# Attention of the first two blocks moved ahead of the first layer's products, with outputs and scores of a visit in PSUM banks of their own

## The chip, the core and the metric

The kernel runs on one core of a Trainium2 chip. The metric is device time in microseconds (us) of one execution; the times shown for the kernel before are a median of three runs and a profile of one more execution.

## What is computed

Three layers follow each other. A retention attention over 4 batches, 8 heads, 768 positions and a head size of 64 gives 3072 tokens of 512 features. A first MLP takes them through `w_in` (512 x 2048) and `w_out`, a second through `w_in2` (512 x 1024) and `w_out2`:

```python
state = gamma * state + k_t (outer) v_t;  y_t = scale * q_t @ state     # attention, per head
h = x @ w_in;   x1 = (h - tanh(h)) @ w_out                              # first MLP
h = x1 @ w_in2; solu = h * softmax(h); out = (layernorm(solu) * g_ln) @ w_out2
```

All inputs are 4-byte floats, but the weights come as 8-byte words that the kernel has to turn into floats itself.

## The kernel before

**Blocks and units.** The sequence is cut into 6 blocks of 128 positions. A block has 4 units, one for each batch, so there are 24 units. A unit holds 8 heads; its recurrence is done by chunks of 64 positions, as products of 64x64 tiles on TensorE. Unit k needs: scores of q and k (`sc`), the growth of the state from k and scaled v (`gn`), the product of q with the old states (`fr`), and the product of the masked scores with scaled v (`y`). Each of the four has 16 products. The trace shows one 64x64 product as two matmul records and two weight loads.

**A visit.** `unit(ko, ks)` (L228) does the outputs `fr` and `y` of one unit, `ko`, and the scores and growth of a later unit, `ks`. It takes four PSUM banks, `one` (two) and `two` (two). In the kernel before each bank holds a half for the outputs and a half for the scores: `one` has `fr` and `sc`, `two` has `y` and `gn`. `prepare(k)` (L207) scales v (`vs`) and q (`qs`, on GpSimd, L223). With `early` the eight scalings of v are on ScalarE (L214), otherwise one is on GpSimd (L218). After the products VectorE makes `pr` (masked scores, L278), `sb` and `sa` (states, L274 and L282), ScalarE copies `fr` to `xf` (L292), VectorE adds `y` to it (L295), and `split_x` (L302) splits the sum into a rounded part `xh` (ScalarE, L307) and a rest `xl` (L308).

**First MLP.** All products of the MLPs are 128x128 by 128x512 and come three to one: high by high, high by low, low by high. `products_h(s, f)` (L313) makes 12 of them for block s and tile f of `w_in` (16 tiles). `less_tanh` (L324) takes the tanh on ScalarE and `g = h - tanh(h)` on VectorE. `products_y` (L338) has 12 products for a tile of `w_out`. A weight tile is decoded in four stages (`Decoder`, L149): its load (`raw`, L116), an absolute value on ScalarE (L122), four operations on VectorE (L129 to L136), and a rounding on ScalarE with a subtraction on VectorE (L145, L146). Decoded tiles stay in SBUF.

**The order around the change.** Units 0 to 3 come first, with two tiles of `w_in` decoded between them. Then a loop over n (L408) does block 0's products for tile n, and block 1's, `BEHIND` = 5 tiles later:

```python
less_tanh(products_h(0, n, ps_y, "y"), g2[n][:, 0, :])          # block 0
if n <= B: ... unit(k - 1 ..., k ..., True)                     # units 4 to 7
elif LATER <= n <= LATER + B: ... unit(..., True, True)         # units 8 to 11
if n >= BEHIND: less_tanh(products_h(1, f, ps_y, "y"), g2[f][:, 1, :])
```

After that loop come the `products_y` of both blocks (L460), the blocks 2 to 5 one by one (L490), and the second MLP (L586). A scheduler puts the instructions of each engine in a fixed order when the program is built; each engine takes its own in that order. The loads `z` (inputs of the units) and `raw` are issued by SyncE (SP), the tables `tab` by ScalarE. Buffers come from pools: 44 of one size (`t4`: `z`, `raw`, decoded weights, x, g), 17 of a smaller one (`t2`).

Of the kernel before, what the change touches and what calls it, by code (L numbers as in the profile page):

```python
# [36 lines left out]
P = 128  # L37
# [11 lines left out]
BEHIND = 5  # L49
LATER = 6  # L50
# [42 lines left out]
def body(ctx: ExitStack, tc, z, w_in, w_out, w_in2, w_out2, g_ln, cst, tab, out):  # L93
# [89 lines left out]
    zero = cpool.tile([P, NP, D], F32, name="zero")  # L183
# [23 lines left out]
    def prepare(k, early):  # L207
        c = k // B
        v = t2([P, H, D], F32, "vs")
        src = zv[k][:, 1, :, :].rearrange("q p (h d) -> q (p h) d", h=2)  # L210
        c0 = C_VS + c * H
        if early:
            for h in range(H):
                nc.scalar.activation(  # L214
                    v[:, h, :], src[:, h, :], AF.Copy, scale=con[:, c0 + h : c0 + h + 1]
                )
        else:
            nc.gpsimd.tensor_tensor(  # L218
                v, src, con[:, c0 : c0 + H].unsqueeze(2).to_broadcast([P, H, D]), ALU.mult
            )  # L220
        vs[k] = v
        qs[k] = t2([P, NP, P], F32, "qs")
        nc.gpsimd.tensor_tensor(  # L223
            qs[k].rearrange("q p t -> q (p t)"),
            zq[k][:, 0, :, :].rearrange("q p t -> q (p t)"), tb[c][1], ALU.mult,
        )

    def unit(ko, ks, early, hold=False, pool=ps_r, tag="r"):  # L228

        if ks is not None:  # L230
            c = ks // B
            if ks not in vs:
                prepare(ks, early)
            kq, kv, v = zq[ks], zv.pop(ks), vs[ks]

        one = [pool.tile([P, 2, 4 * D], F32, tag=tag, name="one") for _ in range(2)]
        two = [pool.tile([P, 2, 4 * D], F32, tag=tag, name="two") for _ in range(2)]
        if ko is not None:
            q, vo, po, st = qs.pop(ko), vs.pop(ko), pt.pop(ko), (sa.pop(ko), sb.pop(ko))
            fr = [t[:, 0, :].rearrange("q (i t) -> q i t", i=2) for t in one]  # L240
            y = [t[:, 0, :].rearrange("q (h i t) -> q h i t", h=2, i=2) for t in two]
            products([
                (
                    fr[h][rows(col(2 * i + odd, h)), i, rows(ab)],
                    st[ab][rows(h), 2 * i + odd, :], q[rows(h), 2 * i + odd, rows(ab)],
                )
                for i in range(2) for ab in range(2) for odd in range(2) for h in range(2)
            ])
        if ks is not None:
            sc, gn = ([t[:, 1, :].rearrange("q (p t) -> q p t", p=NP) for t in w] for w in (one, two))  # L250
# [9 lines left out]
        if ko is not None:  # L260
            products([
                (
                    y[ab][rows(col(p, h)), h, p // 2, :], vo[rows(ab), 2 * p + h, :],
                    po[rows(ab), h, p, :],
                )
                for p in range(NP) for ab in range(2) for h in range(2)
            ])
        if ks is not None:
            sb[ks] = stp.tile([P, NP, D], F32, tag="sb", name="sb", bufs=3)
            if c == 0:  # L270
                sa[ks] = zero
                nc.scalar.copy(sb[ks], gn[0])
            else:
                nc.vector.tensor_tensor(sb[ks], sa[ks], gn[0], ALU.add)  # L274
# [4 lines left out]
            pt[ks] = pr  # L279
            if c < NC - 1:  # L280
                sa[ks + B] = stp.tile([P, NP, D], F32, tag="sa", name="sa")
                nc.vector.tensor_tensor(sa[ks + B], sb[ks], gn[1], ALU.add)  # L282
        if ko is not None:
            c, b = divmod(ko, B)
            if hold:
                if b % 2 == 0:
                    xc[b // 2] = t4([P, 2, 2, 2, P], F32, "xc")
                xf = xc[b // 2][:, b % 2, :, :, :]
            else:
                xf = t2([P, 2, 2, P], F32, "xf")  # L290
            for h in range(2):
                nc.scalar.copy(xf[:, h, :, :], fr[h])  # L292
            xa = xf.rearrange("q h i t -> q (h i) t")
            for ab in range(2):
                nc.vector.tensor_tensor(  # L295
                    xa[:, :, rows(ab)], xa[:, :, rows(ab)],
                    y[ab].rearrange("q h i t -> q (h i) t"), ALU.add,
                )
            if not hold:
                split_x(c, b, xf, nc.vector if early else nc.gpsimd)  # L300

    def split_x(c, b, xf, eng):  # L302
        if b == 0:
            xt[c] = [[t4([P, 2, SB], F32R, f"x{n}") for _ in range(2)] for n in "hl"]
        for h in range(2):
            xh, xl = (xt[c][n][h][:, :, b * P : (b + 1) * P] for n in range(2))
            nc.scalar.copy(xh, xf[:, h, :, :])  # L307
            eng.tensor_tensor(xl, xf[:, h, :, :], xh.bitcast(F32), ALU.subtract)  # L308
# [74 lines left out]
    spare = dict(pool=ps_y, tag="y")  # L383
    dec1.n = NF1
    load_units(1)
    nc.sync.dma_start(out=con, in_=cst[:, :C_IDENT])
    dec1.to(0, 1)
    load_units(4)
    dec1.to(0, 2)
    load_units(5)  # L390
    dec1.to(0, 3)
    nc.gpsimd.memset(zero, 0.0)
    unit(None, 0, True)
    for st in range(1, 4):
        dec1.to(st, 1)
    unit(None, 1, True, **spare)
    prepare(2, True)
    unit(0, 2, True)
    prepare(3, True)
    unit(1, 3, True, **spare)  # L400
    unit(2, None, True)
    dec1.to(1, 2)
    prepare(4, True)
    unit(3, None, True, **spare)
    for st in range(1, 4):
        dec1.to(st, 2)
    g2 = {}
    for n in range(NF1 + BEHIND):  # L408
        if n < NF1:
            while dec1.at[3] < n + 1:  # L410
                dec1.step()
            g2[n] = t4([P, 2, SB], F32, "g")
            less_tanh(products_h(0, n, ps_y, "y"), g2[n][:, 0, :])

        if n <= B:
            k = B + n
            load_units(min(k + 2, 2 * B))
            if n < B - 1:
                prepare(k + 1, True)
            unit(k - 1 if n else None, k if n < B else None, True)  # L420
        elif LATER <= n <= LATER + B:
            k = 2 * B + n - LATER
            load_units(min(k + 2, 3 * B))
            unit(k - 1 if n > LATER else None, k if n < LATER + B else None, True, True)
        elif n == LATER - 1:
            load_units(2 * B + 1)
            nc.sync.dma_start(out=gl, in_=g_ln)
        if n >= BEHIND:
            f = n - BEHIND
            less_tanh(products_h(1, f, ps_y, "y"), g2[f][:, 1, :])  # L430
        if n < NF1 - 3:
            dec1.step()
        else:

            dec1.n = 2 * NF1
            for st, ahead in enumerate((1, -1, -1, -2)):
                dec1.to(st, max(NF1, NF1 + min(4 - st, n - NF1 + 3 + ahead)))
            if n < NF1:
                dec1.to(3, min(NF1, n + 2))
# [6 lines left out]
    split_g(0)  # L446
    py2 = [
# [3 lines left out]
    for n in range(NF1 + 1):  # L451
# [9 lines left out]
        if n % 2 == 0 and NF1 // 2 <= n < NF1:  # L461
            b = (n - NF1 // 2) // 2
            split_x(2, b, xc[b // 2][:, b % 2, :, :, :], nc.vector)
# [26 lines left out]
    for n, (s, f) in enumerate(steps):  # L490
# [4 lines left out]
        if n in visits:  # L495
            unit(*visits[n], False)
            load_units((visits[n][1] or NU) + 2)
# [156 lines left out]
```

## Time and profile before

| | |
|---|---|
| median of 3 runs | 921.95 us (919.96 to 922.29) |
| the profiled execution | 922.72 us, of it 920.8 us in the profile's span |
| TensorE matmul busy | 885.1 us, 96% of the span; 6720 matmuls and 6720 weight loads |
| VectorE, ScalarE, GpSimd busy | 440.4, 307.6, 182.8 us |
| share of TensorE in the chain that ended last | 93% |
| mean granted TensorE clock | 0.983 |
| DMA | 73.48 MB, mean 80 GB/s |

The chain that ended last is followed back from the last instruction, at each step to what released it. A wait named "issue" is one for which the profile shows no releaser. PE is TensorE, DVE VectorE, ACT ScalarE, POOL GpSimd, SP SyncE. A matmul's shown duration overlaps the next one's, so costs of matmuls are taken from a stretch and its count.

### The profile page before, as it was taken

Reading aid. Unit: us, or ns where it says so; the run is one execution under the profiler, and the core shown is the slowest. Engines: PE = TensorE matmul, PEld = TensorE weight load, DVE = VectorE, ACT = ScalarE, POOL = GpSimd, SP = SyncE. Lnnn points to the kernel's source line nnn. Section 1 sums busy time; section 2 is a strip of 40 time slices with the busy share of each in tenths; the row PEclk is TensorE's granted clock in tenths of the full one; section 3 lists DMA queues with packets and bytes.
Section 4 is the critical chain, followed back from the end, with each engine's and each line's share of the span. In section 5 each row is a group of like instructions: output and inputs, shape, how many; then the busy total and the mean of one; then the engine's idle time right before and its main releaser. Section 6 shows DMA issues by size and latency. Waiting matters only on the chain.

```text
span 920.8 us, 16028 instructions
## 1 busy us (share of the span) xinstructions
PE 885.1 (96%) x6720; PEld 728.1 (79%) x6720; DVE 440.4 (48%) x884; ACT 307.6 (33%) x633; POOL 182.8 (20%) x185
## 2 busy tenths in 40 slices
PE   4678999999999999999999999999999999999998
PEld 4555788788888888888888888888888888888886
DVE  3596865996122333222322249973544444444442
ACT  4553633654011121111211133531533333333332
POOL 2101100000024433333333310010222222222210
PEclk9787999999999999999999999999999999999999
DMA  9905112532141123112311026305111111000000
GB/s 358 397 7 183 52 44 69 161 92 92 29 132 47 48 70 95 44 47 69 92 48 46 24 76 199 92 12 142 42 46 46 47 46 47 23 23 23 24 23 35
DMA packets 35640, 73.48 MB, mean 80 GB/s; under 512 B 3184, under 2 KB 15600, under 8 KB 35568
## 3 DMA queue, kind: packets, MB, share of 16 engines
q1 hardware_dynamic: 17712, 56.73, 18.5%
q10 hardware_dynamic: 17856, 15.73, 5.3%
q8 instruction: 53, 0.87, 0.4%
q14 instruction: 19, 0.16, 0.1%
HBM read 59.86 MB, written 12.58 MB: 79 GB/s over the span
## 4 chain that ended last, share of the span: by engine, by line
PE 93%; DVE 3%; ACT 2%; DMA 1%; issue 1%; SPq 0%; ACTq 0%; DVEq 0%
PE py L344 29%; PE ph L320 28%; PE po L578 14%; PE ph L530 14%; PE one L204 2%; PE ptr L565 2%; PE two L204 2%; ACT vs L214 1%; DMA con<-cst 1%; DVE wf L136 1%; DVE xf L295 1%; ACT xf L292 0%; DVE wf L133 0%; DVE wf L129 0%; DVE w L146 0%
## 5 line engine op out<-in xcount | busy, mean ns | idle before, releaser
L320 PE MATMUL ph<-xh,w 128*128 128x512 f32 x768 | 254.2, 400 | 10.4 <-ACT xh L307 5.4
L344 PE MATMUL py<-gh,w 128*128 128x512 f32 x768 | 248.4, 391 | 1.2 <-ACT gh L332 1.2
L320 PEld LDWEIGHTS ph<-xh,w 128*128 128x128 f32 x768 | 147.6, 193 | 42.9 <-ACT xh L307 5.7
L344 PEld LDWEIGHTS py<-gh,w 128*128 128x128 f32 x768 | 144.1, 188 | 31.7 <-ACT gh L332 1.6
L327 DVE TENSOR_TENSOR g<-ph,th 128x512 f32<-128x512 f32 x96 | 66.2, 689 | 204.5 <-ACT th L326 204.2
L320 PE MATMUL ph<-xl,w 128*128 128x512 f32 x384 | 153.1, 399 | 0.0
L344 PE MATMUL py<-gl,w 128*128 128x512 f32 x384 | 150.8, 393 | 0.0
L326 ACT ACTIVATE th<-ph 128x512 f32<-128x512 f32 x96 | 57.4, 598 | 246.8 <-PE ph L320 227.1
L530 PE MATMUL ph<-w,y 128*128 128x512 f32 x576 | 134.9, 389 | 0.0
L530 PEld LDWEIGHTS ph<-w,y 128*128 128x128 f32 x576 | 108.0, 188 | 22.4
L335 POOL TENSOR_TENSOR gl<-g,gh 128x512 fp32r<-128x512 f32 x48 | 61.7, 1286 | 307.9 <-DVE gh L334 286.7
L578 PE MATMUL po<-w,uh 128*128 128x512 f32 x384 | 120.4, 395 | 0.0
L379 POOL TENSOR_TENSOR y<-yl,y 128x512 fp32r<-128x512 f32 x24 | 42.2, 1760 | 260.9 <-ACT y L378 232.5
L320 PEld LDWEIGHTS ph<-xl,w 128*128 128x128 f32 x384 | 74.0, 193 | 15.7
L536 DVE TENSOR_REDUCE nmx<-ph 128x1 f32<-128x1024 f32 x24 | 29.4, 1225 | 117.7 <-PE ph L530 117.7
L344 PEld LDWEIGHTS py<-gl,w 128*128 128x128 f32 x384 | 72.1, 188 | 15.2
L578 PEld LDWEIGHTS po<-w,uh 128*128 128x128 f32 x384 | 70.6, 188 | 13.6
L578 PE MATMUL po<-w,ul 128*128 128x512 f32 x192 | 75.3, 392 | 0.0
L539 ACT ACTIVATE ex<-ph,nmx 128x1024 f32<-128x1024 f32 x24 | 26.8, 1117 | 132.5 <-DVE nmx L536 132.5
L223 POOL TENSOR_TENSOR qs<-z,tab 128x512 f32<-128x512 f32 x24 | 31.9, 1331 | 86.5 <-DMA tab<-tab 36.4
L541 DVE SCALAR_TENSOR_TENSOR ex<-ph,ex 128x1024 f32<-128x1024 f32 x24 | 29.4, 1225 | 29.8 <-ACT ex L539 29.8
L578 PEld LDWEIGHTS po<-w,ul 128*128 128x128 f32 x192 | 36.0, 188 | 7.6
(64 smaller groups left out, 850.7 us busy)
## 6 DMA issues: line engine op xcount, KB each, us to landing
z<-z SPq DMA_DIRECT2D x48, 512.0 KB, 5.8
raw<-w_in SPq DMA_DIRECT2D x24, 512.0 KB, 7.5
raw<-w_out SPq DMA_DIRECT2D x24, 512.0 KB, 3.6
y1d<-ysb ACTq DMA_DIRECT2D x24, 256.0 KB, 3.3
yl<-y1d SPq DMA_DIRECT2D x24, 256.0 KB, 3.3
out<-ob ACTq DMA_DIRECT2D x24, 256.0 KB, 2.1
tab<-tab ACTq DMA_DIRECT2D x12, 256.0 KB, 3.3
ident<-cst SPq DMA_DIRECT2D x1, 64.0 KB, 9.4
```

The lines of the kernel that those rows point to most:

```text
L204: nc.tensor.matmul(o, a, b, start=True, stop=True, skip_group_check=True)
L223: nc.gpsimd.tensor_tensor(qs[k].rearrange("q p t -> q (p t)"), zq[k][:, 0, :, :].rearrange("q p t -> q (p t)"), tb[c][1], ALU.mult,)
L320: nc.tensor.matmul(ph, a[:, k, :], x, start=n == 0, stop=n == 3 * NK - 1)
L326: nc.scalar.activation(th, ph, AF.Tanh)
L327: nc.vector.tensor_tensor(g, ph, th, ALU.subtract)
L335: eng_l.tensor_tensor(gl_, g, gh.bitcast(F32), ALU.subtract)
L344: nc.tensor.matmul(py[e], a[:, cols], x, start=f == 0 and n == 0, stop=f == NF1 - 1 and n == 2)
L379: nc.gpsimd.tensor_tensor(yo, t, yh.bitcast(F32), ALU.subtract)
L530: nc.tensor.matmul(ph[:, half, :], a[:, k, :], b, start=n == 0, stop=n == 3 * NK - 1)
L536: nc.vector.tensor_reduce(nmx, phf, AX.X, ALU.max, negate=True)
L541: nc.vector.scalar_tensor_tensor(ex, phf, 1.0, ex, ALU.mult, ALU.mult, accum_out=us)
L578: nc.tensor.matmul(po, a[:, f, :], b, start=n == 0, stop=n == 3 * NF2 - 1)
```

## The change

All eight units of blocks 0 and 1 run before the loop over the tiles of `w_in`. Then each step n of the loop has both blocks' products for tile n, with units 8 to 11 in steps 3 to 7 (`LATER` = 3). Only the products of block 0 with tile 0 stand earlier, between the units 3 and 4. A visit now puts outputs and scores into banks of their own: `out` (two, with `fr` and `y`) and `sc` (two, with `sc` and `gn`), does the outputs first, and up to unit 7 the score banks come from the pool `ps_y`. Of the first block's units the product with the zero state is gone (8 of 64 products in a unit, with the tile of zeros). For units 0 to 7 half of v's scaling moves from ScalarE to GpSimd, and one of two `xl` from VectorE to GpSimd. In `split_x`, `engs` names an engine for each half. Cut to its core:

```diff
-BEHIND = 5
-LATER = 6
+LATER = 3
...
-    def prepare(k, early):
+    def prepare(k, own):
...
+        for h in range(own):
+            nc.scalar.activation(
+                v[:, h, :], src[:, h, :], AF.Copy, scale=con[:, c0 + h : c0 + h + 1]
+            )
+        if own < H:
             nc.gpsimd.tensor_tensor(
-                v, src, con[:, c0 : c0 + H].unsqueeze(2).to_broadcast([P, H, D]), ALU.mult
+                v[:, own:, :], src[:, own:, :],
+                con[:, c0 + own : c0 + H].unsqueeze(2).to_broadcast([P, H - own, D]), ALU.mult,
             )
...
-    def unit(ko, ks, early, hold=False, pool=ps_r, tag="r"):
+    def unit(ko, ks, hold=False, pool=ps_r, tag="r", engs=None):
...
-        one = [pool.tile([P, 2, 4 * D], F32, tag=tag, name="one") for _ in range(2)]
-        two = [pool.tile([P, 2, 4 * D], F32, tag=tag, name="two") for _ in range(2)]
         if ko is not None:
...
+            w = [ps_r.tile([P, 2, 4 * D], F32, tag="r", name="out") for _ in range(2)]
+            fr = [t[:, 0, :].rearrange("q (i t) -> q i t", i=2) for t in w]
+            y = [t[:, 1, :].rearrange("q (h i t) -> q h i t", h=2, i=2) for t in w]
+
+            steps = range(2) if c else (1,)
...
+            else:
+                for h in range(2):
+                    nc.scalar.copy(xf[:, h, :, rows(1)], fr[h][:, :, rows(1)])
+                nc.scalar.copy(xa[:, :, rows(0)], ya[0])
...
         if ks is not None:
-            sc, gn = ([t[:, 1, :].rearrange("q (p t) -> q p t", p=NP) for t in w] for w in (one, two))
+            c = ks // B
+            kq, kv, v = zq[ks], zv.pop(ks), vs[ks]
+            w = [pool.tile([P, 2, 4 * D], F32, tag=tag, name="sc") for _ in range(2)]
+            sc, gn = ([t[:, n, :].rearrange("q (p t) -> q p t", p=NP) for t in w] for n in range(2))
...
+    both = dict(engs=(nc.vector, nc.gpsimd))
...
+    for k in range(2 * B):
+        load_units(min(k + 6, 2 * B))
+        if k + 2 < 2 * B:
+            prepare(k + 2, H // 2)
+        if k == B:
+            step_h(0, 0)
+        unit(k, k + 2 if k + 2 < 2 * B else None, **both, **(spare if k < B else {}))
+        if k >= B:
+            dec1.to(0, k - B + 2)
+    dec1.step()
+    nc.sync.dma_start(out=gl, in_=g_ln)
+    for n in range(NF1):
+        while dec1.at[3] < n + 1:
+            dec1.step()
+        for b in range(2):
+            if n or b:
+                step_h(n, b)
+
+        if LATER <= n <= LATER + B:
...
```

`step_h(n, b)` is `less_tanh(products_h(b, n, ps_y, "y"), g2[n][:, b, :])`.

**TensorE at the start.** `ph` are products with `w_in`; `one<-qs` and `two<-pr` (before), `out<-qs` and `out<-pr` (now) are outputs; rows from `z` are scores and growth. Before, from the outputs of units 2 and 3 on:

```order
L204 MATMUL two<-pr,vs 64x64 x16
L204 MATMUL one<-qs,zero 64x64 x4
L204 MATMUL one<-qs,sb 64x64 x4
L204 MATMUL one<-qs,zero 64x64 x4
L204 MATMUL one<-qs,sb 64x64 x4
L204 MATMUL two<-pr,vs 64x64 x16
L320 MATMUL ph<-xh,w 128x512 x2
L320 MATMUL ph<-xl,w 128x512
```

Now, from the outputs of unit 3 and the scores of unit 5 on:

```order
L202 MATMUL out<-qs,sb 64x64 x8
L202 MATMUL out<-pr,vs 64x64 x16
L202 MATMUL sc<-z 64x64 x16
L202 MATMUL sc<-vs,z 64x64 x16
L319 MATMUL ph<-xh,w 128x512
L319 MATMUL ph<-xl,w 128x512
```

Twelve `ph` follow there, then the outputs of unit 4; and after the outputs of unit 7 the dense stream of `ph` begins:

```order
L202 MATMUL out<-qs,sb 64x64 x4
L202 MATMUL out<-qs,sa 64x64 x4
L202 MATMUL out<-qs,sb 64x64 x4
L202 MATMUL out<-pr,vs 64x64 x16
L319 MATMUL ph<-xh,w 128x512 x2
L319 MATMUL ph<-xl,w 128x512
```

Units 4 to 7 moved ahead of all `ph` but twelve.

**ScalarE at the end of the units.** `vs` is v's scaling, `xf` and `xh` belong to a unit's outputs, `wf` and `w` to the decoding of `w_in`, `th` is the first tanh. Before, around units 2 and 3, the end of block 0:

```order
L292 COPY xf<-one 128x256
L122 ACTIVATE wf<-raw 128x512
L214 ACTIVATE vs<-z,con 128x64 x4
L292 COPY xf<-one 128x256
L214 ACTIVATE vs<-z,con 128x64 x4
L145 CAST w<-wf 128x512
L307 CAST xh<-xf 128x2x128 x2
L292 COPY xf<-one 128x256 x2
L307 CAST xh<-xf 128x2x128 x2
L326 ACTIVATE th<-ph 128x512
```

Now, at the end of block 1, from the scaling for unit 7 on:

```order
L212 ACTIVATE vs<-z,con 128x64 x4
L262 COPY xf<-out 128x256 x2
L306 CAST xh<-xf 128x2x128 x2
L262 COPY xf<-out 128x256 x2
L306 CAST xh<-xf 128x2x128 x2
L262 COPY xf<-out 128x256
L121 ACTIVATE wf<-raw 128x512 x3
L262 COPY xf<-out 128x256
L306 CAST xh<-xf 128x2x128 x2
L144 CAST w<-wf 128x512 x2
```

Where one decoding stood beside unit 2's copies, the starts of three stand between the two copies of unit 7's outputs.

**SyncE's loads at the start.** Before:

```order
L194 DMA z<-z 128x1024 x2
L386 DMA con<-cst 128x49
L116 DMA raw<-w_in 128x1024
L194 DMA z<-z 128x1024 x6
L116 DMA raw<-w_in 128x1024
L194 DMA z<-z 128x1024 x2
L116 DMA raw<-w_in 128x1024
```

Now, in the same queue, after the first five units' loads and one `raw`:

```order
L192 DMA z<-z 128x1024 x6
L115 DMA raw<-w_in 128x1024 x6
L192 DMA z<-z 128x1024 x4
L115 DMA raw<-w_in 128x1024
L192 DMA z<-z 128x1024 x2
```

The inputs of all eight units stand ahead of the second tile of `w_in`.

## Rows read from the trace of the kernel before

**Rows 1.** Chain of waits in order of time: start, us, what.

```profile
79.53 6.91 PE ph L320 x17
...
121.52 43.76 PE ph L320 x192
165.30 0.60 ACT th L326
...
166.46 87.33 PE py L344 x384
...
282.70 1.09 PE one L204 x64
...
284.92 1.09 PE two L204 x64
```

**Rows 2.** Busy time in stretches: length, engines (instructions), clock, DMA share, GB/s.

```profile
0.00:10.00 10.00, 1.45 (x37) 1.27 (x40) 0.76 (x2) 2.00 (x4) 1.77 (x6) 1.00 0.84 295
10.00:42.00 32.00, 19.89 (x494) 17.82 (x493) 17.45 (x36) 17.56 (x62) 7.87 (x6) 0.79 1.03 406
60.00:70.00 10.00, 8.32 (x192) 6.83 (x182) 9.20 (x21) 5.31 (x18) 0.00 (x0) 1.00 0.01 3
80.00:90.00 10.00, 10.00 (x61) 7.47 (x60) 3.62 (x4) 0.54 (x2) 2.40 (x2) 0.73 0.92 358
```

**Rows 3.** Timeline, TensorE: the two waits that nothing in the profile released.

```profile
26.75 0.27 PE L204 MATMUL two<-vs,z 64*64 64x64 f32 x2 [2.25 <-issue]
33.23 0.38 PE L204 MATMUL one<-qs,sb 64*64 64x64 f32 x4 [3.33 <-issue]
```

**Rows 4.** Busy time as in rows 2, from the start to each wait.

```profile
0.00:24.60 24.60, 11.50 (x348) 10.63 (x349) 8.39 (x14) 11.74 (x40) 7.11 (x10) 1.00 0.96 361
0.00:29.95 29.95, 14.66 (x474) 13.69 (x475) 11.97 (x24) 14.01 (x48) 8.38 (x11) 0.96 0.97 369
```

**Rows 5.** DMA queues: whole span, then 16 to 17, 24 to 26, 30 to 32 us.

```profile
q8 instruction: 53, 0.87, 0.4%
...
q8 instruction: 1, 0.02, 6.8%
...
q8 instruction: 1, 0.02, 3.4%
...
q8 instruction: 1, 0.02, 3.3%
```

**Rows 6.** Groups by line and shape: count, busy us, mean ns, idle before.

```profile
L307 ACT CAST xh<-xf 128x256 fp32r<-128x256 f32 x40 | 14.3, 404 | 33.3 <-DVE xf L295 28.6 <-DMA tab<-tab 4.7
L292 ACT COPY xf<-one 128x256 f32<-128x256 f32 x40 | 13.6, 371 | 54.4 <-DVE pr L278 32.4 <-POOL vs L218 18.6 <-PE one L204 3.3
L122 ACT ACTIVATE wf<-raw 128x512 f32<-128x512 f32 x48 | 31.4, 668 | 9.7 <-PE py L344 8.8 <-DVE w L146 0.9
L146 DVE TENSOR_TENSOR w<-wf,w 128x512 fp32r<-128x512 f32 x48 | 35.7, 743 | 2.0 <-ACT w L145 1.7
L129 DVE TENSOR_SCALAR wf<-wf 128x512 f32<-128x512 f32 x48 | 21.8, 455 | 9.3 <-ACT wf L122 9.3
L327 DVE TENSOR_TENSOR g<-ph,th 128x512 f32<-128x512 f32 x96 | 66.2, 689 | 204.5 <-ACT th L326 204.2
L295 DVE TENSOR_TENSOR xf<-xf,two 128x256 f32<-128x256 f32 x40 | 15.7, 414 | 3.2 <-ACT xf L292 3.2
L218 POOL TENSOR_TENSOR vs<-z,con 128x512 f32<-128x512 f32 x12 | 12.5, 1043 | 0.0
L308 POOL TENSOR_TENSOR xl<-xf,xh 128x256 fp32r<-128x256 f32 x24 | 17.2, 736 | 27.0 <-ACT xh L307 27.0
L223 POOL TENSOR_TENSOR qs<-z,tab 128x512 f32<-128x512 f32 x24 | 31.9, 1331 | 86.5 <-DMA tab<-tab 36.4 <-PE two L204 22.0 <-DVE w L146 11.9
```

**Rows 7.** Timeline, ScalarE, VectorE and GpSimd: v's scalings, then two that overlap.

```profile
9.28 2.02 ACT L214 ACTIVATE vs<-z,con 128x64 f32<-128x64 f32 x8
...
16.51 1.27 POOL L223 TENSOR_TENSOR qs<-z,tab 128x512 f32<-128x512 f32 x1 [1.05 <-DMA z<-z]
16.69 1.64 DVE L146 TENSOR_TENSOR w<-wf,w 128x512 fp32r<-128x512 f32 x1 [0.68 <-ACT w L145]
```

More of the change, by code (lines that the diff above doesn't have):

```diff
@@ L226, in prepare @@
         )
-    def unit(ko, ks, early, hold=False, pool=ps_r, tag="r"):
[L230 to L234, printed above, removed]
-        one = [pool.tile([P, 2, 4 * D], F32, tag=tag, name="one") for _ in range(2)]
-        two = [pool.tile([P, 2, 4 * D], F32, tag=tag, name="two") for _ in range(2)]
-        if ko is not None:
-            q, vo, po, st = qs.pop(ko), vs.pop(ko), pt.pop(ko), (sa.pop(ko), sb.pop(ko))
-            fr = [t[:, 0, :].rearrange("q (i t) -> q i t", i=2) for t in one]
-            y = [t[:, 0, :].rearrange("q (h i t) -> q h i t", h=2, i=2) for t in two]
+    def unit(ko, ks, hold=False, pool=ps_r, tag="r", engs=None):
+        if ko is not None:
+            c, b = divmod(ko, B)
+            q, v, po, st = qs.pop(ko), vs.pop(ko), pt.pop(ko), (sa.pop(ko, None), sb.pop(ko))
+            w = [ps_r.tile([P, 2, 4 * D], F32, tag="r", name="out") for _ in range(2)]
+            fr = [t[:, 0, :].rearrange("q (i t) -> q i t", i=2) for t in w]
+            y = [t[:, 1, :].rearrange("q (h i t) -> q h i t", h=2, i=2) for t in w]
+            steps = range(2) if c else (1,)
             products([
@@ L259, in unit @@
             ])
[L260 to L274, printed above, removed]
             pr = t2([P, 2, NP, D], F32, "pr")
@@ L279, in unit @@
             pt[ks] = pr
+            sb[ks] = stp.tile([P, NP, D], F32, tag="sb", name="sb", bufs=3)
+            if c == 0:
+                nc.scalar.copy(sb[ks], gn[0])
+            else:
+                nc.vector.tensor_tensor(sb[ks], sa[ks], gn[0], ALU.add)
             if c < NC - 1:
@@ L282, in unit, with split_x @@
                 nc.vector.tensor_tensor(sa[ks + B], sb[ks], gn[1], ALU.add)
[L283 to L302, printed above, removed]
+    def split_x(c, b, xf, engs):
         if b == 0:
@@ L386, in body @@
     nc.sync.dma_start(out=con, in_=cst[:, :C_IDENT])
+    load_units(2)
     dec1.to(0, 1)
-    load_units(4)
-    dec1.to(0, 2)
     load_units(5)
-    dec1.to(0, 3)
-    nc.gpsimd.memset(zero, 0.0)
-    unit(None, 0, True)
+    prepare(0, H // 2)
+    unit(None, 0, **spare)
+    prepare(1, H // 2)
     for st in range(1, 4):
         dec1.to(st, 1)
[L396 to L406, printed above, removed]
+    unit(None, 1, **spare)
     g2 = {}
[L408 to L411, printed above, removed]
+    def step_h(n, b):
+        if b == 0:
             g2[n] = t4([P, 2, SB], F32, "g")
[L413 to L421, printed above, removed]
+        less_tanh(products_h(b, n, ps_y, "y"), g2[n][:, b, :])
@@ L422, in body @@
             k = 2 * B + n - LATER
+            if n == LATER:
+                load_units(k + 1)
+                prepare(k, H)
             load_units(min(k + 2, 3 * B))
[L424 to L431, printed above, removed]
+            if n < LATER + B - 1:
+                prepare(k + 1, H)
@@ L432, in body @@
+            unit(k - 1 if n > LATER else None, k if n < LATER + B else None, True)
+        if n < NF1 - 4:
             dec1.step()
@@ L435, in body @@
             dec1.n = 2 * NF1
[L436 to L439, printed above, removed]
+            m = n - (NF1 - 4)
+            for st, ahead in enumerate(((1, 2, 2, 2), (0, 1, 2, 2), (0, 1, 1, 2), (0, 0, 1, 2))):
+                dec1.to(st, max(NF1 if st < 3 else min(NF1, n + 2), NF1 + ahead[m]))
     gs = {}
@@ L495, in body @@
         if n in visits:
-            unit(*visits[n], False)
-            load_units((visits[n][1] or NU) + 2)
+            ko, ks = visits[n]
+            if ks is not None:
+                prepare(ks, 0)
+            unit(ko, ks)
+            load_units((ks or NU) + 2)
             next_y(n)
```

38 lines of the change are left out of this document (28 added, 10 removed).

## The prediction

> **What bounds the kernel now.** I read the chain of waits in order of time first, then the busy time by stretches, then the waits of TensorE and the DMA queues in the first 50 us. In the chain [rows 1] the reader is to see one point: from 79.53 us on it is TensorE's own work almost without a break, through the last product with `w_in` (its tanh starts at 165.30) and the products with `w_out`. 192 products took 43.76 us, 0.228 us each, and a unit's outputs and scores 1.09 + 1.09 = 2.18 us. That work is the same after the change, so time can only come out of the stretch before 79.5 us, where TensorE waits, or be lost there.
>
> What it waits for before 79.5 us has two parts. From 60 to 70 us VectorE is busy 9.20 of 10 us [rows 2]: the decoding of `w_in`, the units 4 to 7 and their splits meet on VectorE while each step gives TensorE work for one block only. Before that, from 10 to 42 us, the DMA engines are full (share 1.03, 406 GB/s [rows 2]), and TensorE stops twice, 2.25 and 3.33 us, for nothing that the profile shows, in the middle of a unit's products [rows 3]. At the first stop it had executed 348 matmuls and 349 weight loads, at the second 474 and 475 [rows 4]: 697 and 949, 252 apart. The queue named q8 moved 53 packets and 0.87 MB in all [rows 5], 16.4 KB each, for TensorE's 6720 matmuls and 6720 weight loads: one packet for 254 of these 13,440. So I read the stops as TensorE waiting for its own instructions: one packet stands in 16 to 17 us, one in 24 to 26 and one in 30 to 32 us [rows 5]. TensorE went on at 26.75 and 33.23, 6.48 us apart. A unit is 64 products, 128 matmuls and 128 weight loads: **one packet per unit, and 6.5 us for it while the loads fill the DMA engines.** This is an inference; no row names the cause of the stop.
>
> **The change part by part.**
>
> *Both blocks in each step.* Per tile of `w_in` TensorE now has 24 products, 24 x 0.228 = 5.5 us, where VectorE needs the decoding (two operations like L129's 0.455, three no longer than L146's 0.743: 3.1) and two subtractions of 0.689 [rows 6]: 4.5 us. VectorE's bound goes away, and with it the stretch like 60 to 70 us. In steps 3 to 7 a unit adds 2.18 us on TensorE and about 2.5 us on VectorE (six operations like L295's 0.414): 7.7 against 7.0, still TensorE.
>
> *The dense stream.* Let S be the time at which unit 7's x is split and the stream can start. What is left then is 2 x 16 x 12 - 12 = 372 products (twelve ran between the units), 372 x 0.228 = 84.8 us, and four units, 4 x 2.18 = 8.7 us. TensorE comes out of a pause and starts at the lower of its two clock levels: from 80 to 90 us the granted clock was 0.73 [rows 2], 27% of 10 us, and with the half us before it 2.9 us lost. I take the same. The products with `w_in` then end at S + 96.4, against 165.3 now: **the saving is 68.9 - S.** The 755 us behind are taken as unchanged.
>
> *The units: TensorE's instructions.* This sets S. Units 0 to 3 lose 8 products, 32 instructions each; up to the end of unit 7 there are 8 x 256 - 128 + 24 = 1944. The blocks of 256 begin, by the stops at 697 and 949, at 441, 697, 953, 1209, 1465 and 1721. The one of 441 came with the packet of 16 to 17 us and could be used some 2.5 us later, as at the other two stops, at 18.5. At 6.5 us for each: 25.0, 31.5, 38.0, 44.5, 51.0. Unit 6's outputs (1688 to 1816) hold 1721, so they end at about 51.9 if nothing gets easier. The DMA engines stay full up to about 40 us: ahead of the first load that waits for a freed buffer stand 27 loads of 0.524 MB and four tables of 0.262, 15.2 MB; 2.95 in the first 10 us (295 GB/s) and the rest at 406 GB/s [rows 2] end at 40.2. If the last two packets then cost nothing, unit 6's outputs end at about 45.5, by ScalarE's order. The truth lies between 45.5 and 51.9; I take 49.4, on the late side, since loads that wait for buffers of the units follow.
>
> *From unit 6's outputs to S.* ScalarE copies (2 steps, 0.65), VectorE adds (0.4), `xh` (0.7), the first copy of unit 7 (0.35), then three `wf` (1.85), the second copy (0.3), two adds (0.7), `xh` (0.7), all from the groups' means less the overlap that the timeline shows in runs of two or three [rows 6]; last VectorE's `xl`, which stands behind four decoding steps (2.1) and takes 0.4, beside GpSimd's `xl` (0.736). Sum 8.15; some 0.5 of it overlaps, so 7.6. S = 49.4 + 7.6 = **57.0**. Bounds: 53.1 and 59.5.
>
> *ScalarE, VectorE and GpSimd in the units.* They have to stay under 6.5 us a unit to cost nothing. ScalarE: four scalings instead of eight, 1.0 (eight took 2.02 [rows 7]), a state copy below 0.4, outputs 0.65 to 0.8 (three copies, two of them half as long as L292's 0.371 or, at most, as long), `xh` 0.7 and the wait for VectorE between, 3.3 to 3.5 us. GpSimd: half of `vs`, which no row shows, between half of 1.043 and all of it [rows 6], near the half; 1.331 and 0.736 added: 2.6 to 3.1. VectorE 1.9 to 2.7. A subtraction of SBUF tiles on VectorE was held up by a GpSimd operation, 1.64 us where it takes 0.74 [rows 7, 6]; each unit has one such `xl`, at most 1 us, inside the slack. If TensorE's packets came at once this slack would be the path (first rival).
>
> *The banks.* Before a visit takes four banks at one time, and a score cannot overwrite its bank until the outputs in the other half are read. Now these are apart. In the dense stretches TensorE has no idle time to give back; in the units it waits for its packets. I cost it at nothing, between 0 and -1 us.
>
> *The zero products and memset.* 32 products, the 128 instructions that are taken off above.
>
> *The switch to `w_out`.* At the last product with `w_in` the big buffers hold 16 weight tiles, 16 g, 8 x, 2 held x and two decoded `w_out` tiles: all 44. The third `w_out` can only be loaded when block 0's x is free; load, decoding and casts take 8 to 12 us against 10.9 us of products (48 x 0.228) in the first two tiles. 0 to 1 us; I take 0, as the buffers come free 2.7 us before the last product.
>
> Sum: 68.9 - 57.0 = 11.9 us saved. The profiled execution took 922.72 us, 1.9 more than its span of 920.8; it would be 910.8. It stands 0.8 above the median, so against the median **910.0 us**.
>
> **The rivals.**
>
> *The instructions are no bound, ScalarE's order is.* For it: the stops are only two, and TensorE may have waited for something else that the profile doesn't record. ScalarE's 3.4 us a unit from unit 0's copies at about 17 us give block 0's x at 30.0, the twelve products to 33.9, unit 6's outputs at 40.2 and S at 49.5: a saving of 19.4 us, **902.5 us**. Against it: nothing that the profile shows held TensorE at 24.5 and 29.9 us. [...]
>
> *Each packet takes longer, and the change is slower.* The spacing of packets from 16 to 24 us was 8, not 6.5. With all loads of eight units queued one behind the other, five spacings after 18.5 decide: S = 18.5 + 5 x spacing + 8.5. From 7.8 us on (S = 66.0) the change is within 0.3%, from 8.9 us on (S = 71.5) **slower**; at 9.5 us S is 74.5 and the time 927.6. Against it: from 16 to 24 us TensorE had other waits, and the two clean spacings are 6.5.
>
> *VectorE stays the bound in the dense stream.* With 7.0 against 7.7 us in steps 3 to 7 it would have to lose 0.8 us a step to GpSimd's `qs`, 1.331 us [rows 6]. Where it does, some 0.5 us in each of four steps: 912.0 us.
>
> **How the numbers follow.** Forecast (S from 53 to 61, 906 to 914 us): 0.57. Instructions no bound, 902.5: 0.18. VectorE in the dense stream, 912: 0.05. Longer packets: same 0.08, slower 0.05. The remaining 0.07 are other cases that are still faster. 0.3% is 2.8 us, about what a measurement can tell from no change. Faster 0.87, same 0.08, slower 0.05. The range takes in the first rival at its low end and spacings up to 7.3 us (S = 63.5) at its high end: 901 to 917.
>
> **What would show it.** TensorE's waits named "issue" should stand four to six times in the first 52 us, some 256 instructions apart, and the q8 packets some 6.5 us. Block 0's x should be complete near 35, the dense stream of `ph` start near 57 and its last tanh near 153.4, with no wait over 2 us between, and the first product with `w_out` follow within 2 us. No "issue" waits and a start at 50 would prove the first rival; a start after 66 the second. VectorE at over 90% in steps 3 to 7 would speak for the third. A gap behind the last tanh would show the buffers mis-costed.

## The result and the profile after

The kernel after takes **910.87 us** (median of 4 runs, 910.23 to 911.3); the kernel before, on the same chip, 921.59 us (4 runs, 919.96 to 922.29). The ratio is 0.9886, with a 95% interval of 0.9868 to 0.9903. The forecast was 910.0, its range 901 to 917. The span went from 920.8 to 908.8 us.

First TensorE's waits up to 75 us in the kernel after (engine, tile and line, what it waited for: us in all, times, longest). Two stops named "issue" [rows 3] have become four, 8.5 and 2.7 us in all:

```profile
PE out L202 <- issue: 8.5, 3, 3.2
PE sc L202 <- DMA z<-z: 5.4, 1, 5.4
PE ph L319 <- ACT xh L306: 4.9, 1, 4.9
PE sc L202 <- ACT vs L212: 4.2, 4, 3.3
PE sc L202 <- issue: 2.7, 1, 2.7
```

The chain in order of time (start, us, what), the answer to [rows 1]:

```profile
21.34 2.66 issue
27.69 2.58 issue
33.30 3.29 PE ph L319 x12
39.66 3.16 issue
46.35 2.73 issue
49.08 1.13 PE out L202 x53
...
57.02 4.35 POOL xl L307
...
154.14 0.60 ACT th L325
...
155.30 87.34 PE py L343 x384
```

TensorE went on at 24.00, 30.27, 42.82 and 49.08 us: 6.27, two times 6.28, and 6.26 apart. The last tanh of the products with `w_in` starts at 154.14, where it was 165.30: 11.16 us of the 12.0 are there. What lies behind it is 908.8 - 154.14 = 754.66 us, against 755.50.

How much TensorE had executed at each stop is the count in windows from 0 to the stop (us, then PE and PEld busy with their counts, DVE, ACT, POOL, granted clock, DMA share, GB/s), as in [rows 4]:

```profile
0.00:21.40 21.40, 11.54 (x347) 10.21 (x348) 6.99 (x17) 9.21 (x30) 8.02 (x13) 1.00 0.95 354
0.00:27.75 27.75, 15.23 (x474) 13.70 (x474) 9.75 (x23) 12.73 (x43) 11.22 (x16) 0.91 0.97 367
0.00:39.70 39.70, 24.19 (x726) 21.10 (x727) 14.79 (x37) 17.73 (x60) 16.30 (x22) 0.87 0.98 379
0.00:46.40 46.40, 27.72 (x852) 24.44 (x853) 17.45 (x44) 20.20 (x68) 18.82 (x25) 0.86 0.99 383
```

347 + 348 = 695, then 948, 1453 and 1705. Before, the stops came at 697 and 949. **A different program, and it stops at the same counts of its own instructions**; 1453 lies twice 252 behind 948. The one between, near 1201, was reached only at 36.7 us, behind the twelve products of `ph` (1187 at 36.60), when its packet was due at 36.55 by the spacing: no stop.

The queue q8 [rows 5] agrees. In windows of 0.25 us its packets stand at 21.25, 27.50, 33.75, 40.00 and 46.25 us. Four of them come 2.5 to 2.8 us before TensorE goes on; the one at 33.75 is that of the boundary which was reached late. The next two, at 50.00 and 53.50, follow 3.75 and 3.5 us after the one before, while the loads end.

The loads last longer than forecast. From 46 to 52 us the DMA engines still have a share of 0.63, so they are full to about 50 us:

```profile
46.00:52.00 6.00, 3.04 (x127) 2.66 (x126) 2.50 (x7) 1.42 (x5) 0.72 (x1) 0.78 0.63 248
```

### The profile page after: what moved, and what is told of

Same layout as the page of the kernel before. It is cut to its first block, busy times and chain, and to the rows that moved or that the text cites. A ratio compares the mean times of both kernels' runs of the same rounds, so it can differ in the third digit from the quotient of the medians.

```text
span 908.8 us, 15882 instructions
## 1 busy us (share of the span) xinstructions
PE 876.0 (96%) x6656; PEld 724.9 (80%) x6656; DVE 429.9 (47%) x872; ACT 300.7 (33%) x605; POOL 195.9 (22%) x200
## 4 chain that ended last, share of the span: by engine, by line
PE 90%; issue 3%; DVE 2%; POOL 2%; ACT 2%; DMA 1%; POOLq 0%; DVEq 0%; ACTq 0%
PE ph L319 29%; PE py L343 26%; PE po L580 14%; PE ph L532 14%; PE ptr L567 2%; PE sc L202 2%; PE out L202 2%; POOL vs L216 1%; DVE g L326 1%; ACT th L325 1%; DMA z<-z 1%; POOL xl L307 1%; DMA tab<-tab 1%; DVE gh L333 0%; DVE xf L268 0%
## 5 line engine op out<-in xcount | busy, mean ns | idle before, releaser
L319 PE MATMUL ph<-xh,w 128*128 128x512 f32 x768 | 248.1, 392 | 5.3 <-ACT xh L306 4.9
L319 PEld LDWEIGHTS ph<-xh,w 128*128 128x128 f32 x768 | 144.7, 188 | 36.5 <-ACT xh L306 5.3
L319 PE MATMUL ph<-xl,w 128*128 128x512 f32 x384 | 150.3, 391 | 0.1
L334 DVE TENSOR_TENSOR gl<-g,gh 128x512 fp32r<-128x512 f32 x48 | 33.7, 708 | 8.8 <-PE py L343 5.5
```

The source lines that it names most:

```text
L319: nc.tensor.matmul(ph, a[:, k, :], x, start=n == 0, stop=n == 3 * NK - 1)
L334: eng_l.tensor_tensor(gl_, g, gh.bitcast(F32), ALU.subtract)
```

## The experiments

All are changes of the kernel after, except e10_visit_alone, which is one of the kernel before. "Start" is the first product of the dense stream of `ph` behind unit 7 (before: 79.53), "behind" is the span less the start of the last tanh. Ratios are to the kernel before, in the same set of runs. e2_half computes attention in lower precision, so its time is no gain.

| | median us | ratio, 95% interval | stops over 1 us | start | last tanh | behind |
|---|---|---|---|---|---|---|
| after | 910.87 | 0.9886 (0.9868 to 0.9903) | 4 | 56.69 | 154.14 | 754.7 |
| e1_gate | 908.30 | 0.9853 (0.9832 to 0.9874) | 2 | 51.33 | 151.98 | 754.5 |
| e2_half | 879.28 | 0.9540 (0.9522 to 0.9559) | 0 | 44.40 | 139.94 | 738.0 |
| e3_pad | 915.37 | 0.9935 (0.9916 to 0.9953) | 5 | 61.36 | 159.34 | 754.6 |
| e4_scale_act | 912.05 | 0.9897 (0.9880 to 0.9915) | 4 | 57.84 | 155.57 | 754.8 |
| e5_gate_once | 904.95 | 0.9825 (0.9809 to 0.9841) | 2 | 50.60 | 148.06 | 755.2 |
| e6_tail | 907.63 | 0.9856 (0.9840 to 0.9871) | 4 | 54.49 | 151.71 | 754.5 |
| e7_gate_tail | **901.60** | 0.9791 (0.9776 to 0.9806) | 2 | 48.37 | 145.49 | 754.5 |
| e8_banks | 921.65 | 1.0007 (0.9997 to 1.0016) | 4 | 58.73 | 160.62 | 760.5 |
| e9_order_alone | 917.15 | 0.9958 (0.9942 to 0.9975) | 4 | 61.76 | 160.36 | 755.5 |
| e10_visit_alone | 915.23 | 0.9941 (0.9926 to 0.9956) | 0 | 73.08 | 158.29 | 754.5 |
| e11_zero | 913.34 | 0.9917 (0.9902 to 0.9932) | 5 | 58.72 | 156.16 | 754.5 |

**Are the stops the loads' doing?** A copy of one element into a tile that a load then overwrites makes the load wait for the copy's source (in the kernel below SyncE's queue waited for one such copy for up to 24.4 us). For the loads issued behind units 2 and 3 that is the sum of this unit, for those behind unit 7 its sum; the loads `z` have the same line. Three more tiles of `w_in` are loaded ahead of that:

```diff
+    def hold_back(t):
+        if gate[0] is not None:
+            nc.gpsimd.tensor_copy(t, gate[0])
     def raw_load(src):
         raw = t4([P, 512, 2], I32, "raw")
+        hold_back(raw[:, 0, 0:1].bitcast(F32))
...
+        if 2 <= k <= 4:
+            dec1.to(0, k)
         load_units(min(k + 6, 2 * B))
...
-        if k >= B:
-            dec1.to(0, k - B + 2)
+        gate[0] = xfs[k] if 2 <= k < 4 else None
+    nc.gpsimd.tensor_copy(mark, xfs[2 * B - 1])
+    gate[0] = mark
     dec1.step()
```

> The loads that the first eight units do not need (all but four tiles of w_in, and block 2's z) wait until unit 7's outputs are read; TensorE's instructions stay as they are. Theory (TensorE waits for its own instructions, and the loads make each packet slow): the last load before that point ends near 30 us, so of the four stops named issue the two behind it (that ended at 42.82 and 49.08) vanish or fall below 1 us; the dense stream of ph starts at 50 to 52 us instead of 56.69, and the time is 904 to 906.5 us. Rival (the stops have nothing to do with the loads): four stops of 2.6 to 3.2 us as before, the stream starts at 56.7 or, with decoding that now starts later, 58, and the time is 910.5 to 913 us.

The first stretch below has the last inputs of the units, the second no loads to speak of:

```profile
28.00:34.00 6.00, 4.08 (x104) 3.65 (x105) 2.59 (x9) 2.81 (x12) 3.12 (x6) 0.50 0.54 181
34.00:40.00 6.00, 5.73 (x141) 4.51 (x139) 2.13 (x6) 1.44 (x4) 1.84 (x3) 0.84 0.18 70
```

TensorE's own rows with an "issue" wait are then two, at the old places, and the start is 5.4 us earlier:

```profile
23.93 0.38 PE L212 MATMUL sc<-vs,z 64*64 64x64 f32 x3 [2.49 <-issue]
29.92 0.38 PE L212 MATMUL out<-qs,sb 64*64 64x64 f32 x3 [2.30 <-issue]
...
51.33 0.80 PE L330 MATMUL ph<-xh,w 128*128 128x512 f32 x1 [4.72 <-ACT xh L317]
```

The two stops behind 30 us are gone, as the theory said, and the packets of q8 that the kernel after has at 33.75 and 40.00 us stand at 31.00 and 35.25. The time is outside what either expected, 908.3: 3.2 us were lost again behind the start. The next kernel holds back one load only:

```diff
             nc.gpsimd.tensor_copy(t, gate[0])
+            if gate[0] is mark:
+                gate[0] = None
```

> As e1_gate, but only the first load behind unit 7 is held back by GpSimd; all later ones follow it in SyncE's order without a copy of their own. In e1_gate the stream started at 51.33 instead of 56.69, and 3.2 of these 5.4 us were lost again by the last tanh (100.6 us after the start, where the changed kernel needs 97.5), 2.2 of them at 88 us, where ScalarE's scaling of block 2 stood in front of a cast. Theory (that loss is the copies' doing: z of block 2 came late): the stream starts at 51 to 51.6 us, no wait over 1 us is left between 52 and 150 us, the last tanh stands at 148.6 to 149.5 us, the time is 904.5 to 906 us. Rival (the loss is a later stage's bound, which any earlier start meets): the last tanh stays at 151 to 152 us and the time at 907.5 to 908.5.

The start is 50.60, the last tanh 148.06: now 6.1 us earlier both times, and 904.95 us. The loss in the gate with many copies was the copies' own.

**Are the packets TensorE's instructions?** Half of the attention's instructions, then 256 more:

```diff
+            a, b = (
+                t.bitcast(mybir.dt.bfloat16).rearrange("p (n t) -> p n t", t=2)[:, :, 1]
+                for t in (a, b)
+            )
```

> The 64x64 products of attention read only the upper 16 bits of their fp32 inputs, so attention is computed in lower precision; a product is then one matmul and one weight load instead of two and two. Loads are unchanged. Theory (one packet per 256 instructions): up to the end of unit 7 TensorE needs about 970 instructions instead of 1944, so at most two boundaries lie in the units after the first and are reached after their packets; no stop named issue over 1 us is left, the units go by ScalarE's order, and the dense stream starts at 49 to 51.5 us. Rival (the stops are not the instructions): the stops stay where they were, in time, and the stream starts at 55 us or later. The whole time also falls by what the shorter products save in units 8 to 23, at most 2.18 us in each of 16, so it lies between 870 and 905 us and says little by itself; stops and start decide.

With the loads as they were, no wait named "issue" is left in the first 75 us, and the units now wait for ScalarE's scaling, the longest group:

```profile
PE sc L206 <- ACT vs L216: 9.8, 6, 4.0
PE sc L206 <- DMA z<-z: 7.4, 3, 6.1
PE ph L323 <- ACT xh L310: 3.8, 2, 3.3
```

The start, 44.40, is 4.6 us below the lowest that was expected. Shorter products in the units may be part of that; it was not separated. The packets of q8 over the whole span, in the kernel after, in this one and in the next:

```profile
q8 instruction: 52, 0.85, 0.4%
...
q8 instruction: 40, 0.66, 0.3%
...
q8 instruction: 53, 0.87, 0.4%
```

They go with TensorE's matmuls and weight loads: 13,312, 10,304 and 13,568 of these, one packet for 256, 258 and 256.

```diff
+            if c == 0:
+                products(2 * [
+                    (
+                        fr[h][rows(col(2 * i + odd, h)), i, rows(0)],
+                        st[1][rows(h), 2 * i + odd, :], q[rows(h), 2 * i + odd, rows(0)],
+                    )
+                    for i in range(2) for odd in range(2) for h in range(2)
+                ])
```

> Units 0 to 3 get 16 more products each, whose results nobody reads: 64 products, 128 matmuls and 128 weight loads, 256 instructions, one packet more. As work they are 64 x 0.017 = 1.1 us of TensorE in all, which was idle for more than that in each unit. Theory (instructions): unit 6's outputs now need one more packet, so a fifth stop appears behind the one that ended at 49.08; the stream starts 2.5 us later if that packet is fast because the loads have ended by then, 6.3 us later if it keeps the spacing: 59.2 to 63.0 us, and 913 to 917.5 us. Rival (products as work, no packets): the stream starts 0 to 1.1 us later, 911 to 912 us.

The stop that was expected behind 49.05 is there, though only 0.83 us long: TensorE went on at 53.02, 3.97 us later, between the two spacings that were given. The packets at counts 443 and 1204, which had come in time in the kernel after, were now reached too early as well (stops of 1.15 and 2.68 us), while the one at 1453 came in time. The start moved 4.67 us for products that are worth 1.1. The counts at the last two stops, in windows as above:

```profile
0.00:46.20 46.20, 26.01 (x854) 23.39 (x855) 14.82 (x37) 17.80 (x60) 16.29 (x22) 0.82 0.98 381
0.00:52.25 52.25, 29.16 (x980) 26.35 (x981) 17.46 (x44) 20.27 (x68) 18.81 (x25) 0.81 0.94 365
```

1709 and 1961. The padded program has other products there than the kernel after, and its stop at 1709 lies within 4 of that one's 1705.

The number of the zero products alone:

```diff
-                products(2 * [
+                products([
```

> The changed kernel with the zero products' number of instructions put back: eight more products in each of units 0 to 3, 32 in all, 128 instructions, results unread. In e3_pad 256 instructions brought one stop more, usable 4.0 us after the one before, and moved the start by 4.7 us. Theory (blocks of 256): the boundary behind 1721, at 1977, now falls into unit 7's outputs, which wait for a packet until 53.1 and end at 53.9 instead of 51.8; the start moves by 0.5 to 2 us, to 57.2 to 58.7, and the time is 911 to 913 us. Rival (cost goes with the number of instructions, not with blocks): half of e3_pad's, 2.3 us, 59.0 and 913.2 us. Rival (work only): 0.5 us at most.

The start moved by 2.03 us, to the edge of what the theory gave and as near to the rival's 2.3, so this does not tell them apart. The way was another than expected: unit 7's outputs had no stop. Stops came on top at the counts 443 (1.13 us, from 16.46 to 17.59) and 1202 (2.51 us), the one at 696 grew to 4.03 us, and the one at 1453 is gone. Only the price is shown: 2.0 us for 128 instructions.

**Is ScalarE's order the path?**

```diff
-            prepare(k + 2, H // 2)
+            prepare(k + 2, H)
```

> All eight heads' scalings of v of units 0 to 7 on ScalarE instead of four there and four on GpSimd: 1.0 us more of ScalarE in each unit. Theory (a unit takes a packet's 6.3 us, of which ScalarE uses some 3.5): nothing in units 0 to 7, the dense stream starts 0 to 1 us later than 56.69 and the time is 910.5 to 912 us. Rival (ScalarE's order is the path through the units): 1.0 us in each of up to eight units, start at 61 to 65 us, 915 to 919 us.

The start is 1.15 us later, a little over the theory's 1, for some 8 us more of ScalarE: the rival fell. Most of a unit's 6.3 us was slack for ScalarE.

**The rest of the way to the start.** Unit 7's copies, adds and casts are pinned ahead of the decoding of three tiles, which the scheduler had put between them:

```diff
-                    nc.scalar.copy(xf[:, h, :, :], fr[h])
+                    kept(ko)(nc.scalar.copy(xf[:, h, :, :], fr[h]))
...
+        i = nc.scalar.activation(wf, raw[:, :, 1].bitcast(F32), AF.Abs)
+        if step0[0]:
+            tc.keep_in_program_order(i)
...
+    def kept(k):
+        return tc.keep_in_program_order if k == 2 * B - 1 else lambda i: i
```

> The changed kernel with one thing different: unit 7's copies, adds and casts stand ahead of the decoding of three w_in tiles on ScalarE and VectorE, no load is held back. Theory (behind the packets, the rest of the way to the stream is unit 7's chain on ScalarE and VectorE, lengthened by three wf and some decoding steps): the four stops stay, unit 7's xh follows at 53.8 to 54.6 us, the stream starts there, 2 to 2.9 us earlier than 56.69, waits up to 1 us for the second tile's decoding, and the time is 908 to 909.5 us. Rival (the decoding itself is what the stream needs, so its delay costs as much as it gives): the gain is lost at the second tile, 910.5 to 911.5 us.

And with the edits of e5_gate_once and e6_tail together:

> e5_gate_once and e6_tail together. Theory (loads that slow the packets, and the order behind the last unit, are two separate parts of the start): start at 47.3 to 48.6 us, waits of up to 1.5 us for the decoding of the second and third tile, time 901.5 to 904 us. Rival (the decoding is what the stream needs, now that the units end at 45): no better than e5_gate_once, 904.5 to 906 us.

Pinning alone moved the start by 2.2 us and the last tanh by 2.4; with the gate, 8.3 and 8.65 us. Both together give 901.60 us, the fastest of the kernels here that compute in full precision, 1% below the changed one. The decoding was not what the stream needed first. One row shows more than the order: GpSimd's last `xl`, in the kernel after and then in e6_tail:

```profile
57.02 4.34 POOL L307 TENSOR_TENSOR xl<-xf,xh 128x256 fp32r<-128x256 f32 x1 [3.76 <-ACT xh L306]
```

```profile
54.82 0.73 POOL L316 TENSOR_TENSOR xl<-xf,xh 128x256 fp32r<-128x256 f32 x1 [1.41 <-ACT xh L315]
```

Beside VectorE's decoding it took 4.34 us, ahead of it 0.73. In those 4.34 us VectorE worked with no pause over 0.1 us, seven operations of 0.42 to 0.69 us and the start of an eighth.

**The banks and the order.** Outputs and scores go into the same banks again; units 0 and 2 also take theirs from `ps_r`, as before the change:

```diff
+        w1, w2 = ([pool.tile([P, 2, 4 * D], F32, tag=tag, name=m) for _ in range(2)] for m in ("one", "two"))
-            fr = [t[:, 0, :].rearrange("q (i t) -> q i t", i=2) for t in w]
-            y = [t[:, 1, :].rearrange("q (h i t) -> q h i t", h=2, i=2) for t in w]
+            fr = [t[:, 0, :].rearrange("q (i t) -> q i t", i=2) for t in w1]
+            y = [t[:, 0, :].rearrange("q (h i t) -> q h i t", h=2, i=2) for t in w2]
```

> The changed kernel with the outputs and the scores of a visit in halves of the same four banks again, as before the change; the order of all work stays. Theory (in the units TensorE waits for its packets and in the dense stretches its queue holds other work, so the banks give nothing): the stream starts 0 to 1 us later than 56.69 and the time is 910.5 to 912.5 us. Rival (shared banks make a visit's first products wait until VectorE has read the scores of the visit before, 1.5 to 2 us): units 4 to 7, which have only one set of four banks, cost 3 to 6 us, start at 59.7 to 62.7, time 914 to 917 us.

Both were wrong: the whole gain is gone, 921.65 us. The start lost only 2.0 us; 4.4 more went up to the last tanh (101.9 us from the start, against 97.5) and 5.8 behind it. A visit in the later blocks shows where. In the kernel after it is one piece, from 271.48 to the next product with `w_out` at 273.80:

```profile
271.48 0.34 PE L202 MATMUL out<-qs,sa 64*64 64x64 f32 x8
...
272.46 0.65 PE L202 MATMUL sc<-z 64*64 64x64 f32 x32
273.18 0.69 PE L202 MATMUL sc<-vs,z 64*64 64x64 f32 x32
273.80 0.50 PE L343 MATMUL py<-gh,w 128*128 128x512 f32 x1
```

With shared banks the same visit is cut up, and large products stand between its pieces:

```profile
277.94 0.34 PE L202 MATMUL one<-qs,sa 64*64 64x64 f32 x8
...
278.46 0.65 PE L202 MATMUL two<-pr,vs 64*64 64x64 f32 x32
279.04 0.50 PE L342 MATMUL py<-gh,w 128*128 128x512 f32 x1
279.37 0.39 PE L342 MATMUL py<-gl,w 128*128 128x512 f32 x1
279.61 0.40 PE L342 MATMUL py<-gh,w 128*128 128x512 f32 x1
279.93 0.33 PE L202 MATMUL one<-z 64*64 64x64 f32 x4
280.19 0.50 PE L342 MATMUL py<-gh,w 128*128 128x512 f32 x1
280.53 0.40 PE L342 MATMUL py<-gl,w 128*128 128x512 f32 x1
280.86 0.62 PE L202 MATMUL one<-z 64*64 64x64 f32 x26
...
281.94 0.73 PE L342 MATMUL py<-gh,w 128*128 128x512 f32 x2
```

From 277.94 to 281.94 are 4.00 us; less five large products of 0.227 they are 2.87, against 2.32 in one piece. That is 0.55 us for one visit with no wait in TensorE's rows, at a granted clock of 1.00; 5.8 us over 13 later visits are 0.45 each. The visit of the kernel before shares its banks too, and is interrupted once:

```profile
282.63 0.34 PE L204 MATMUL one<-qs,sa 64*64 64x64 f32 x8
...
283.15 0.65 PE L204 MATMUL one<-z 64*64 64x64 f32 x32
283.72 0.50 PE L344 MATMUL py<-gh,w 128*128 128x512 f32 x1
...
284.85 0.69 PE L204 MATMUL two<-vs,z 64*64 64x64 f32 x32
285.36 0.65 PE L204 MATMUL two<-pr,vs 64*64 64x64 f32 x32
285.94 0.50 PE L344 MATMUL py<-gl,w 128*128 128x512 f32 x1
```

These are 3.31 us, less four large products 2.40. The visit in one piece has a wait of its own: 32 small matmuls take 0.47 us there, so those of 272.46 were through near 272.93, and the next, which need GpSimd's scaling of v, came at 273.18. Without that wait it would be some 2.07 us (an estimate from these rows), so one interruption costs some 0.3 us and two cost 0.8. In the rows the time goes at the changes between small and large products: the large ones that start at 280.19 and 280.53 take 0.34 and 0.33 us to the next start instead of 0.227, and the four small ones at 279.93 take 0.26, where 32 take 0.47. For the 4.4 us in the dense stream, where visits are interrupted too, this was not counted; and that the scheduler put products in between because a bank was not yet free is argued, not shown.

Then the visit of before in the new order of the program:

```diff
-            w = [ps_r.tile([P, 2, 4 * D], F32, tag="r", name="out") for _ in range(2)]
...
-            w = [pool.tile([P, 2, 4 * D], F32, tag=tag, name="sc") for _ in range(2)]
...
+        one = [pool.tile([P, 2, 4 * D], F32, tag=tag, name="one") for _ in range(2)]
+        two = [pool.tile([P, 2, 4 * D], F32, tag=tag, name="two") for _ in range(2)]
...
+    nc.gpsimd.memset(zero, 0.0)
```

> The new order of the program with the visit as it was before the change (zero products, shared banks, outputs, scores, then the second half of the outputs). In e8_banks shared banks in the new order of a visit cost 12.3 us of span: 2.0 up to the start, 4.4 in the dense stream and 5.8 behind it, where the visits were cut into pieces between other products. Theory A (the banks matter only together with the new order within a visit; the old order hides them): start 58 to 61 us (shared banks and half a packet for the zero products), behind the last tanh within 1 us of the 755.5 of before, time 912 to 917 us. Theory B (shared banks cost what e8_banks shows in any order): a loss of some 10 us again behind the start, 920 to 926 us.

Theory A holds behind the last tanh, to the digit: 755.5, as before. A later visit is interrupted once again, and takes 3.31 us as before (277.69 to 281.00). The time, 917.15, lies just above what it gave, as does the start of 61.76, 5.1 us later than in the kernel after.

And the new visit in the order of before:

```diff
-        one = [pool.tile([P, 2, 4 * D], F32, tag=tag, name="one") for _ in range(2)]
-        two = [pool.tile([P, 2, 4 * D], F32, tag=tag, name="two") for _ in range(2)]
...
+            w = [ps_r.tile([P, 2, 4 * D], F32, tag="r", name="out") for _ in range(2)]
...
+            w = [pool.tile([P, 2, 4 * D], F32, tag=tag, name="sc") for _ in range(2)]
...
-    nc.gpsimd.memset(zero, 0.0)
```

> The order of the program as before the change, with the new visit (banks of their own, no zero products, all outputs first). The prediction's sum puts all of its 11.9 us into the order. Theory A: the bound of VectorE at 60 to 70 us and the second stream of block 2 steps stay, the visit gives half a packet at most and 0.8 us behind the last tanh: 917.5 to 921 us. Theory B (the new visit is most of the gain, as e8_banks could be read): 910 to 915 us.

915.23 us, between the two. The two stops of before, 2.25 and 3.33 us [rows 3], are gone (no wait named "issue" is over 0.45), and block 0's first product stands at 32.23 instead of 36.69. VectorE is still the bound from 60 to 70 us, as in [rows 2]:

```profile
60.00:70.00 10.00, 8.74 (x214) 6.88 (x212) 9.40 (x23) 4.89 (x13) 0.00 (x0) 1.00 0.01 3
```

By the medians (before: 921.0 in these runs), the visit alone gives 5.8 us and the order alone 3.9, together 9.6 of the 10.7 that the whole change gave in its own runs.

## Why the prediction was right, and where it was not

**Packets set S: right.** The stops stand at the predicted boundaries, counted to within 1% (1453 and 1705 for 1465 and 1721), and the packets come every 6.27 us, where 6.5 was taken. Two stops went when the loads did (e1, e5), all went when the attention's instructions were halved (e2), and more came with 256 more (e3). That a stop is TensorE waiting for its own instructions remains an inference, since no row names it. For it speak the counts, the packets of q8, whose number goes with that of TensorE's instructions (52, 40 and 53), and their place, 2.5 to 2.8 us before the end of each stop; no other cause was found that fits. The four stops are 11.1 us. There was none at the boundary that TensorE reached late (near 1201, 36.7 us), and in e1_gate and e5_gate_once, with loads held back, none over 1 us behind 30.3 us.

**S itself: right by errors that cancel.** Predicted 57.0, measured 56.69. Unit 6's outputs ended at 50.2 instead of 49.4. The packets came earlier than taken, the last at 49.08 instead of 51.0, but the loads fill the DMA engines to about 50 us, not 40.2, and no packet up to then got cheaper. The tail to S was 6.5 us, not 7.6. And x was not complete at S, but when GpSimd's slow `xl` ended at 61.4.

**The dense stream: right in its total.** 154.14 - 56.69 = 97.45 against 96.4. Its low clock at the start (0.50 granted from 52 to 60 us, 1.00 from 61 us on; before the change 0.50 from 79 to 85 and 1.00 from 86 us on) cost less than the 2.9 us taken, 34% of 5.31 us or 1.8:

```profile
56.69:62.00 5.31, 4.88 (x13) 3.29 (x14) 5.13 (x9) 1.49 (x3) 4.34 (x1) 0.66 0.00 0
```

The four units among the products cost more than 8.7: with 84.8 us for the products and 0.3 us of waiting, some 10.5 are left (an estimate). VectorE was no bound: TensorE has no wait over 0.3 us from 58 us to the last tanh. The switch to `w_out` has the same 1.2 us gap as before; a tile's load and decoding, taken as 8 to 12 us, are 7.8 to 9.3 in the trace of before (3.5 to 5.0 us to landing, 4.3 us from 125.00 on). The rivals fell: four stops and a start at 56.69 speak against "ScalarE's order", 6.27 us against slower packets. The first rival's start of 49.5 doesn't follow from its own 40.2 either: the tail of 7.6 us gives 47.8, or 48.7 if the outputs start at 40.2.

**The sum: right in its total, wrong in its parts.** Two terms failed. "I cost it at nothing, between 0 and -1 us", of the banks: undone in the new kernel, they are worth 10.8 us (921.65 against 910.87). TensorE's wait for a bank that is not yet read stands once in the trace of before, 1.77 us at 70.09 (`one<-qs,sa`, for ScalarE's `xf`). The step that failed is "in the dense stretches TensorE has no idle time to give back". That was true, but the price of a bank that is not free was not idle time: the visit was cut into pieces between other products, and each change cost TensorE time. The old visit hid most of this by its own order of products (one interruption where the new one has two; e9), so the banks and the order within the visit have no price apart from each other. And the sum gave all 11.9 us to the order of the program; alone it gives 3.9. The visit alone takes the two stops out of the old order, which the prediction never asked; whether its fewer instructions do that or its banks was not separated. Removing 32 zero products was counted inside S and is 2.0 us of it. The order gives the stream of both blocks but runs eight units against all the loads, which brings two stops more.

## What to carry to other kernels

Where an engine stops in the middle of a run of small instructions and the profile names no releaser, count its instructions up to each stop, over several versions of the program: equal counts (here 697 and 695, 949 and 948) speak for the place in the program and against the data. Then fewer instructions, or loads that are held back until they are needed, can bring more than a better order of the work (here 5.9 us for the held loads against 3.9 for the order alone; fewer instructions were run in lower precision only). And undo a part of a change in the changed kernel as well as doing it alone in the old one: the two can give very different prices.

## What was not expected of the hardware

- Stops at nearly the same counts in the versions counted here: 697 and 949 before; 695, 948, 1453, 1705 after; 1709 and 1961 with 256 instructions more. That is every 252 or 253 recorded instructions, with one q8 packet for 254 to 256 over the whole span.
- A packet of q8 came every 6.3 us while the loads filled the DMA engines, 3.75 and 3.5 us apart as they ended, and 4.25 us apart where they were held back (e1_gate).
- Changes between 64x64 and 128x512 products cost TensorE time that is no wait in its rows: 2.87 us for a visit cut by two pieces of `w_out` products, 0.55 us more than in one piece.
- GpSimd's subtraction of two SBUF tiles took 4.34 us beside VectorE's decoding and 0.73 us without it. It took 4.33 us in e1_gate, again beside decoding, and 0.73 in e7_gate_tail. In the kernel before, three subtractions of VectorE (`w`, L146) that began beside a `qs` of GpSimd took 1.64 [rows 7], 1.77 and 1.50 us, at 16.69, 79.50 and 103.14 us; the other 45 took 0.68 or 0.69. What GpSimd waited for in the 4.34 us is not shown.
